# Attention scores in split float32r, transpositions of a slot first, and a written TensorE order, in a block-attention and gated-MLP kernel

## The chip, the cores and the metric

The kernel runs on one core of one Trainium2 chip. The metric is the device time of one execution in microseconds; lower is better. An execution under the hardware profiler gives the profile and the trace; times are in microseconds unless marked ns.

## The reference

Per batch (8) and head (8), with 576 positions of 64 values, the reference computes attention that is causal by blocks of 64. The eight heads are then laid side by side as 512 features, and a gated MLP with a mix over positions follows.

```python
scores = scale * np.matmul(q, k.transpose(0, 1, 3, 2))
mask = block_i >= block_j
scores = np.where(mask, scores, -1000000000.0)
scores = scores - np.max(scores, axis=-1, keepdims=True)
attn = np.exp(scores)
attn = attn / (np.sum(attn, axis=-1, keepdims=True) + 1e-09)
return np.matmul(attn, v).astype(np.float32)
...
h = x @ w_in
h = 0.5 * h * (1.0 + np.tanh(c * (h + 0.044715 * h ** 3)))
u, v = (h[..., :d_ff // 2], h[..., d_ff // 2:])
v_n = (v - mu) / np.sqrt(var + 1e-06) * g_ln
v_s = np.einsum('ts,bsd->btd', w_sg, v_n) + b_sg[None, :, None]
gated = u * v_s
return (x + gated @ w_out).astype(np.float32)
```

All inputs and outputs are float32, but the MLP's weights, which the kernel converts itself. The host only lays data out: q and k arrive transposed (64 values by 576 positions a head), and the output leaves transposed.

## The kernel before

**Pairs and slots.** Two heads of one batch make a pair, so there are 32 pairs. Their q and k lie one head in partitions 0 to 63 and the other in 64 to 127. One iteration of the last loop (L720) is a slot: it finishes the values' products of pair n (class Values) and makes the scores of pair n + 1 (class Scores). Four slots are one batch.

**Scores.** A pair has five row tiles: tile 0 has 64 rows, tiles 1 to 4 have 128, and tile i sees 64 + 128 i columns. `products` (L280) multiplies in fp32, one product for each head and part; the trace shows each fp32 product as two records, one for each of its two passes over the moving columns. `maximum` (L293) is one VectorE operation that adds the mask, scales, writes the scores to SBUF and takes the row's extreme; `exponent` (L308) is one ScalarE operation that also gives the row's sum. A slot has four score steps (L329 to L339): tile 4's first half with tile 1, tile 4's second half, tile 3 with tile 0, tile 2. Four sets of probability tiles (L149) let two pairs be alive at once.

**Values.** The probabilities are transposed by TensorE against an identity (L353) in three groups a head (`turn0`, `turn2`, `turn1`, L362 to L387), each into one PSUM bank that ScalarE or VectorE copies out (table TE, L341). A diagonal tile is transposed in its lower 64 rows alone, so the tile shape on the array changes there from 128 by 128 to 64 by 128. `turn_sums` (L405) transposes the inverse sums, which POOL has spread over 64 columns a head (L395). The values' products `av0`, `av2`, `av1` (L420 to L435) multiply fp32 values (the stationary operand, 64 columns a head) with the transposed probabilities, for both heads into the two halves of one bank. `normalise` (L437) multiplies by the inverse sums and spills the result; `split` (L445) splits it in a high float32r part and the rest, for the MLP.

**Feed-forward.** The MLP is a chain of generators that yields after each accumulated bank: 5 steps of `v_part` (products of 512 columns), 8 of `u_part`, 8 of `s_part` (the mix over positions) and 8 of `o_part`, all as sums of three float32r products of split operands with 288 columns, but v. `hole(k)` (L643) runs the next k steps; they stand in the slots where TensorE would otherwise have little, by the table PLAN (L660). The order of the parts is v, u, the output of the batch before, s. The norm between v and s (moments, centring, scaling, splitting) is a list of small steps, `side`, that `run_side(k)` (L459) issues k at a time; GELU is one entry of it for `run_gelu`. Weights arrive as 64-bit floats and are taken apart by three VectorE operations (L183, L184, L187), ScalarE and POOL in steps that `load_share` spreads by the table WS (L652).

**What sets the order.** The program is written for a planner: it simulates the engines and issues each engine's instructions in the order in which they become ready by its own costs. `tc.keep_in_program_order` (L82) binds an instruction to the written order; `PIN` (L57) is empty here, so TensorE's instructions are planned freely. PSUM has two rings: five banks "s" for scores, accumulators and outputs, three banks "p" for transpositions. All loads and stores are issued from SP's queue.

## Time and profile before

| | us |
|---|---|
| median of 3 runs | 1051.23 (1049.72 to 1056.15) |
| span of the profiled execution | 1050.8 |
| TensorE, matmuls | 964.7 busy, 5554 records |
| VectorE | 465.9 busy |
| ScalarE | 427.0 busy |
| POOL | 267.4 busy |
| HBM traffic | 45.78 MB read, 18.87 MB written, 62 GB/s over the span |

The profiled execution took 1050.75. "PE" is TensorE's matmuls, "PEld" its weight loads, DVE VectorE, ACT ScalarE, POOL GpSimd, SP the queue that issues the transfers. A tile's name stands with the operand it is written from: `s<-k_f,q_f` is a score product, `ob<-pt,v_f` a values' product, `pa`, `pb`, `pc`, `pd`, `pe` are the banks of transpositions, `accv`, `accu`, `accs` and `acco` the feed-forward accumulators. Matmuls are pipelined, so a record lasts longer than the step from its start to the next one's; the steps are what the engine's time is made of.

### The profile page before, as it was taken

What the parts mean: (1) busy time and instruction counts of PE and PEld (TensorE: products, weight loads), DVE (VectorE), ACT (ScalarE), POOL (GpSimd) and SP (SyncE); (2) the same over time, 40 slices, a digit from 0 to 9 for tenths busy, and PEclk for the clock granted to TensorE, in tenths of its full rate; (3) what the DMA queues carried; (4) which work ended last, traced back from release to release, by engine and by line L of the source; (5) the groups of instructions that cost most, each with busy time, mean ns of one, the idle gap of its engine ahead of it and who ended that gap; (6) DMA issues with size and microseconds to landing.
All of it is one profiled execution on the core that took longest, in us unless ns stands there. A gap on an engine that the chain in (4) does not pass through costs nothing.

```text
span 1050.8 us, 15018 instructions
## 1 busy us (share of the span) xinstructions
PE 964.7 (92%) x5554; PEld 690.3 (66%) x5554; DVE 465.9 (44%) x1442; ACT 427.0 (41%) x1122; POOL 267.4 (25%) x341
## 2 busy tenths in 40 slices
PE   8699999998889988999889998899988999889988
PEld 4245767576657765677666776567765577658978
DVE  6855285427334273342722526434263342723333
ACT  5765662562253622536224263243632536322210
POOL 3621064104212042120420303302042020422232
PEclk7799999998989989899878999889989899869999
DMA  7522111112210122101220112211122011112022
GB/s 233 167 91 68 56 56 46 46 46 68 95 34 31 46 68 90 46 22 46 68 80 34 46 47 68 79 35 46 46 68 88 27 44 58 34 39 75 1 90 68
DMA packets 46908, 65.61 MB, mean 62 GB/s; under 512 B 4082, under 2 KB 22514, under 8 KB 46836
## 3 DMA queue, kind: packets, MB, share of 16 engines
q1 hardware_dynamic: 46836, 64.67, 18.8%
q8 instruction: 43, 0.70, 0.3%
q14 instruction: 29, 0.24, 0.1%
HBM read 45.78 MB, written 18.87 MB: 62 GB/s over the span
## 4 chain that ended last, share of the span: by engine, by line
PE 76%; DVE 13%; ACT 3%; DMA 2%; POOL 2%; issue 2%; SPq 1%; DVEq 0%; POOLq 0%; ACTq 0%
PE s L85 12%; PE accs L85 12%; PE acco L85 11%; PE ob L85 11%; PE accv L85 10%; PE accu L85 9%; PE pc L88 3%; PE pb L88 3%; DVE prob L297 3%; PE pa L88 2%; DVE bs L518 2%; DVE xr L635 2%; ACT prob L310 1%; PE pe L88 1%; DMA w<-in_w_in 1%
## 5 line engine op out<-in xcount | busy, mean ns | idle before, releaser
L310 ACT ACTIVATE prob<-prob,negm 128x448 f32<-128x448 f32 (+3 forms) x320 | 177.8, 556 | 235.5 <-DVE negm L297 234.1
L85 PE MATMUL s<-k_f,q_f 64*128 64x288 f32 (+4 forms) x768 | 193.9, 447 | 34.2 <-DVE negm L297 23.7
L297 DVE CUSTOM_DVE_ANT_0 prob<-s,mask 128x288 f32<-128x288 f32 (+2 forms) x320 | 122.2, 424 | 168.9 <-PE s L85 168.8
L85 PEld LDWEIGHTS s<-k_f,q_f 64*128 64x128 f32 (+1 forms) x768 | 88.9, 188 | 102.1 <-issue 40.3
L85 PE MATMUL ob<-pt,v_f 128*64 128x448 f32 (+4 forms) x640 | 129.5, 454 | 11.0 <-ACT pt L92 6.6
L85 PE MATMUL acco<-gh,wo_h 128*128 128x288 f32 x256 | 94.2, 369 | 19.5 <-DVE xr L635 10.9
L273 POOL MEMSET sums<- 128x2 f32 x32 | 4.3, 137 | 353.1 <-DVE r L392 353.1
L611 POOL TENSOR_TENSOR gl<-u,gh 128x288 fp32r<-128x288 f32 x64 | 51.6, 807 | 154.6 <-DVE gh L610 151.9
L85 PEld LDWEIGHTS ob<-pt,v_f 128*64 128x64 f32 x640 | 44.1, 141 | 69.2 <-issue 39.7
L85 PE MATMUL acco<-gl,wo_h 128*128 128x288 f32 x256 | 87.1, 340 | 0.0
L85 PE MATMUL acco<-gh,wo_l 128*128 128x288 f32 x256 | 86.6, 338 | 0.0
L635 DVE TENSOR_TENSOR xr<-acco,xr 128x288 f32<-128x288 f32 x64 | 29.0, 456 | 121.1 <-PE acco L85 113.5
L85 PEld LDWEIGHTS acco<-gh,wo_h 128*128 128x128 f32 x256 | 58.9, 230 | 31.8 <-DVE xr L635 16.6
L85 PE MATMUL accu<-xh,wi_h 128*128 128x288 f32 x256 | 79.1, 309 | 0.0
L85 PE MATMUL accs<-ws_h,vh 128*128 128x288 f32 x256 | 76.8, 303 | 1.5 <-ACT pt L92 1.5
L85 PE MATMUL accs<-ws_h,vl 128*128 128x288 f32 x256 | 75.9, 297 | 0.0
L85 PE MATMUL accu<-xh,wi_l 128*128 128x288 f32 x256 | 75.5, 295 | 0.0
L85 PE MATMUL accu<-xl,wi_h 128*128 128x288 f32 x256 | 75.4, 295 | 0.0
L85 PE MATMUL accs<-ws_l,vh 128*128 128x288 f32 x256 | 75.1, 294 | 0.0
L85 PE MATMUL accv<-wi_h,xh 128*128 128x512 f32 x160 | 66.0, 413 | 0.0
L92 ACT COPY pt<-pa 128x512 f32<-128x512 f32 x32 | 18.6, 581 | 110.8 <-PE pa L88 110.8
L85 PE MATMUL accv<-wi_l,xh 128*128 128x512 f32 x160 | 63.4, 396 | 0.0
(102 smaller groups left out, 1839.8 us busy)
## 6 DMA issues: line engine op xcount, KB each, us to landing
q_f<-in_qT SPq DMA_DIRECT2D x32, 288.0 KB, 2.9
k_f<-in_kT SPq DMA_DIRECT2D x32, 288.0 KB, 3.2
spill<-x SPq DMA_DIRECT2D x32, 288.0 KB, 3.2
xr<-spill SPq DMA_DIRECT2D x32, 288.0 KB, 2.8
out_T<-xr SPq DMA_DIRECT2D x32, 288.0 KB, 2.1
v_f<-in_v SPq DMA_DIRECT2D x32, 256.0 KB, 3.1
w<-in_w_in SPq DMA_DIRECT2D x16, 256.0 KB, 4.7
w<-in_w_out SPq DMA_DIRECT2D x8, 256.0 KB, 3.9
```

The source lines that it names most:

```text
L85: return pin(nc.tensor.matmul(*a, **k), "P")
L88: return pin(nc.tensor.transpose(out, in_, identity), "P")
L92: return f(dst, src)
L273: nc.gpsimd.memset(self.sm[:, 0, :], 1.0)
L297: nc.vector.tensor_tensor_reduce(self.prob[a][i][r, lo:hi], self.where[a, i, lo], mask[r, MW - (hi - lo) :] if 0 < i and hi == e else mask ...
L310: nc.scalar.activation(self.prob[a][i][r, :e], self.prob[a][i][r, :e], AF.Exp, bias=self.negm[a][r, i : i + 1], scale=-1.0, accum_out=self ...
L518: tc.keep_in_program_order(nc.vector.bn_stats(bs[:rows, :], x))
L611: nc.gpsimd.tensor_tensor(glo[:, ts], x, ghi[:, ts].bitcast(F32), op=ALU.subtract)
L635: nc.vector.tensor_tensor(x[:, ts], acc[:, :SH], x[:, ts], op=ALU.add)
```

## The change

- **Scores.** q and k of a pair are split once (new function `split_qk`) in a high float32r part and a rest. A product is the sum of three float32r products, high by high, rest by high, high by rest, written alternately for the two heads. The split is made by POOL (for the first pair by VectorE and ScalarE). Tile 0 is multiplied with 128 rows instead of 64. The four steps become two: `first` (tile 4's two halves, tiles 1 and 0) and `second` (tiles 3 and 2). There is one set of probability tiles instead of two, and one buffer each for raw and split q and k.
- **Transpositions.** All are 128 by 128. Per head they are grouped in A (tile 4, four column tiles), B and C (five each), and with the sums they stand at the start of the slot, with feed-forward steps between the groups; the scores of the next pair come after them. Of the six copies out, three go to ScalarE and three to VectorE.
- **Values' products.** They come in one visit, between the next pair's two score steps, in 15 pieces a head, one for each pair of row and column tiles, instead of 6.
- **Order and banks.** `PIN` is "P": TensorE runs in the written order. The two PSUM rings become one of eight banks.
- **Plan.** PLAN puts the parts of the MLP in whole slots: v in a batch's first slot, u, the earlier output and s in the next three, four steps of them at the slot's end. `run_side` hands out three steps at a time. WS gives the first four slots 2 weight steps each.

```diff
-    PIN = ""
+    PIN = "P"
...
-    def bank(tag, name, bufs):
-        return psum.tile([P, 512], F32, tag=tag, name=name, bufs=bufs)
...
+    def bank(name):
+        return psum.tile([P, 512], F32, tag="bank", name=name, bufs=8)
...
+    def split_qk(n):
+        out = []
+        for x, t in zip(raw.pop(n), "qk"):
+            hi = sp.tile([P, S], F32R, tag=t + "h", name=t + "h", bufs=1)
+            lo = sp.tile([P, S], F32R, tag=t + "l", name=t + "l", bufs=1)
+            if n == 0:
+                copy("v" if t == "q" else "a", hi, x)
+                nc.vector.tensor_tensor(lo, x, hi.bitcast(F32), op=ALU.subtract)
+            else:
+                copy("g", hi, x)
+                nc.gpsimd.tensor_tensor(lo, x, hi.bitcast(F32), op=ALU.subtract)
+            out += [hi, lo]
+        qk[n] = out
...
-                    mm(dst, self.q[r, QS[i] : QS[i] + n], self.k[r, lo:hi], start=True, stop=True)
+                for y, (q, k) in enumerate(
+                    ((self.qh, self.kh), (self.ql, self.kh), (self.qh, self.kl))
+                ):
+                    for a in (0, 1):
+                        r = slice(a * D, (a + 1) * D)
+                        mm(
+                            t[a][:, cols],
+                            q[r, QS[i] : QS[i] + P],
+                            k[r, lo:hi],
+                            start=y == 0,
+                            stop=y == 2,
+                        )
...
+        def first(self):
             self.step((4, 0, SH), (1, 0, EXT[1]))
+            self.step((4, SH, S), (0, 0, EXT[0]))
+
+        def second(self):
+            self.step((3, 0, EXT[3]))
             self.step((2, 0, EXT[2]))
...
+    TE = {(0, "A"): "a", (1, "A"): "v", (0, "B"): "a", (1, "B"): "v", (0, "C"): "v", (1, "C"): "a"}
+    PLACES = {
+        "A": ((4, 0, 0), (4, 1, 128), (4, 2, 256), (4, 3, 384)),
+        "B": ((4, 4, 384), (3, 3, 320), (3, 2, 256), (3, 1, 128), (3, 0, 0)),
+        "C": ((1, 1, 384), (1, 0, 320), (2, 2, 192), (2, 1, 128), (2, 0, 0)),
+    }
...
+        def turn(self, a, which):
+
+            t = bank("p" + which)
+            for i, j, c in PLACES[which]:
+                turn(t[:, c : c + P], prob[a][i][:, P * j : P * (j + 1)])
+            pt = sp.tile([P, 512], F32, tag="pt", name="pt" + which, bufs=6)
+            copy(TE[a, which], pt, t)
+            for i, j, c in PLACES[which]:
+                self.pt[a, i, j] = pt[:, c + BLK : c + P] if i == j else pt[:, c : c + P]
...
+            t, t2 = bank("pd"), bank("pe")
             for a in (0, 1):
+                turn(t[:, a * BLK : a * BLK + P], prob[a][0])
+            for i in (0, 1, 2):
+                c = 2 * BLK + (i and BLK + P * (i - 1))
+                turn(t[:, c : c + P], spread(i))
+            for i in (3, 4):
+                turn(t2[:, P * (i - 3) : P * (i - 2)], spread(i))
...
+            self.o0 = t2[:, 2 * P : 2 * P + BLK]
+
+        def products(self):
+
+            self.ob = bank("ob")
+            for i in (4, 3, 2, 1, 0):
+                for j in range(i + 1):
+                    c = BLK if i == j and i else 0
+                    w = BLK if i == j else P
+                    c += P * (i - 1)
+                    for a in (0, 1):
+                        r = slice(a * D, (a + 1) * D)
+                        dst = self.ob[r, c : c + w] if i else self.o0[r, :]
+                        mm(
+                            dst,
+                            self.v[:, j, r],
+                            self.pt[a, i, j],
+                            start=j == 0,
+                            stop=j == i,
+                        )
 
         def normalise(self):
 
             x = self.x = page(F32, S, "x")
+            nc.vector.tensor_tensor(x[:, BLK:], self.ob, self.rb[:, BLK:], op=ALU.mult)
             nc.vector.tensor_tensor(x[:, :BLK], self.o0, self.rb[:, :BLK], op=ALU.mult)
-            nc.vector.tensor_tensor(x[:, BLK:], self.ob, self.rb[:, BLK:], op=ALU.mult)
...
-    WS = [2, 5, 7, 8, 3, 2, 1, 1]
+    WS = [2, 2, 2, 2, 8, 2, 2, 2, 4, 4]
...
-    PLAN = ["12211", "12211", "12211", "12222"]
+    PLAN = ["1112", "2114", "2114", "2114"]
...
         va.inverse()
+        va.turn(0, "A")
+        va.turn(1, "A")
         hole(g[0])
+        run_side(3)
         for f in pending:
             f()
         pending.clear()
+        va.turn(0, "B")
+        va.turn(1, "B")
         hole(g[1])
+        run_side(3)
+        load_share(n, 0)
+        va.turn(0, "C")
+        va.turn(1, "C")
+        va.turn_sums()
+        hole(g[2])
         run_gelu()
         load_share(n, 1)
         if nx:
+            nx = Scores(n + 1)
+            nx.first()
+        va.products()
+        va.normalise()
+        if nx:
+            nx.second()
         load_share(n, 2)
+        if n % 4 == 3:
+            va.split()
+        else:
+            pending.append(va.split)
+        if n + 2 < N:
+            split_qk(n + 2)
+        for _ in range(g[3]):
+            hole()
+            run_side(3)
         load_share(n, 3)
```

More of the change, by code (lines that the diff above doesn't have):

```diff
@@ L85, in mm, with turn @@
         return pin(nc.tensor.matmul(*a, **k), "P")
-    def turn(out, in_, identity):
-        return pin(nc.tensor.transpose(out, in_, identity), "P")
+    def turn(out, in_):
+        return pin(nc.tensor.transpose(out, in_, ident), "P")
     def copy(e, dst, src):
@@ L102, in load_qk @@
         b, h = PAIRS[n]
-        q_f = sp.tile([P, S], F32, tag="q_f", name="q_f", bufs=2)
-        k_f = sp.tile([P, S], F32, tag="k_f", name="k_f", bufs=2)
+        q_f = sp.tile([P, S], F32, tag="q_f", name="q_f", bufs=1)
+        k_f = sp.tile([P, S], F32, tag="k_f", name="k_f", bufs=1)
         nc.sync.dma_start(q_f, qT[b, h : h + 2].rearrange("a d s -> (a d) s"))
         nc.sync.dma_start(k_f, kT[b, h : h + 2].rearrange("a d s -> (a d) s"))
-        qk[n] = (q_f, k_f)
+        raw[n] = (q_f, k_f)
+    def split_qk(n):
[11 more added lines that the diff above has]
+        qk[n] = out
     def load_v(n):
@@ L124 @@
     make_identity(nc, ident)
-    t = sbank("warm")
+    t = bank("warm")
     for _ in range(18):
@@ L142 @@
         v_bufs.append(t)
-    pt0 = []
+    prob = []
     for s in (0, 1):
-        t = cp.tile([P, 2 * BLK], F32, name=f"pt0_{s}")
-        nc.gpsimd.memset(t[BLK:, :], 0.0)
-        pt0.append(t)
-    prob = []
-    for s in range(4):
         row = []
         for i in range(NT):
-            t = cp.tile([P, P * (i + 1) if i else BLK], F32, name=f"prob{s}_{i}")
+            t = cp.tile([P, P * (i + 1)], F32, name=f"prob{s}_{i}")
             if i:
                 nc.gpsimd.memset(t[:, EXT[i] :], 0.0)
+            else:
+                nc.gpsimd.memset(t, 0.0)
             row.append(t)
@@ L276, in __init__ @@
             ]
-            self.prob = prob[n % 2 * 2 : n % 2 * 2 + 2]
             self.where = {}
         def products(self, *parts):
-            t = [sbank("s"), sbank("s")]
+            t = [bank("s"), bank("s")]
             off = 0
             for i, lo, hi in parts:
-                n, rows = QN[i], slice(0, QN[i])
+                cols = slice(off, off + hi - lo)
                 for a in (0, 1):
-                    r = slice(a * D, (a + 1) * D)
-                    dst = t[a][rows, off : off + hi - lo]
-                    self.where[a, i, lo] = dst
-                    mm(dst, self.q[r, QS[i] : QS[i] + n], self.k[r, lo:hi], start=True, stop=True)
+                    self.where[a, i, lo] = t[a][: QN[i], cols]
+                for y, (q, k) in enumerate(
[10 more added lines that the diff above has]
+                        )
                 off += hi - lo
@@ L297, in maximum @@
             nc.vector.tensor_tensor_reduce(
-                self.prob[a][i][r, lo:hi],
+                prob[a][i][r, lo:hi],
                 self.where[a, i, lo],
@@ L310, in exponent @@
             nc.scalar.activation(
-                self.prob[a][i][r, :e],
-                self.prob[a][i][r, :e],
+                prob[a][i][r, :e],
+                prob[a][i][r, :e],
                 AF.Exp,
@@ L400, in turn_sums, with spread @@
         def turn_sums(self):
-            t = self.t4 = pbank("pd")
+            def spread(i):
+                return self.rx[:, i, :]
+            t, t2 = bank("pd"), bank("pe")
             for a in (0, 1):
-                turn(t[:BLK, a * BLK : (a + 1) * BLK], self.prob[a][0][:BLK, :BLK], ident[:BLK, :BLK])
-            turn(t[:, 128:256], self.rx[:, 0, :], ident)
-            pt = self.pt0 = pt0[self.n % 2]
-            copy("a", pt[:BLK, :], t[:BLK, : 2 * BLK])
-            self.rb = sp.tile([P, S], F32, tag="rb", name="rb")
@@ L409, in turn_sums @@
-            copy("a", self.rb[:, :BLK], t[:, 128:192])
-            t = pbank("pe")
-            for i in range(1, NT):
-                turn(t[:, (i - 1) * P : i * P], self.rx[:, i, :], ident)
-            copy("a", self.rb[:, BLK:], t)
-        def av(self, dst, j, pts, c0, n, start, stop):
-            for a in (0, 1):
-                r = slice(a * D, (a + 1) * D)
-                mm(dst[r, :], self.v[:, j, r], pts[a][:, c0 : c0 + n], start=start, stop=stop)
-        def av0(self):
-            self.ob = sbank("ob")
-            pt = [self.pt.pop((a, 0)) for a in (0, 1)]
-            self.av(self.ob, 0, pt, 0, 512, True, False)
@@ L477, in accumulator @@
     def accumulator(name):
-        return sbank(name)
+        return bank(name)
     def feed_forward(b):
@@ L490, in v_part @@
         x_s = xs[b]
-        for st in (NT - 1, *range(NT - 1)):
+        for st in range(NT):
             rows = P if st < NT - 1 else TAIL
@@ L507, in v_part @@
             else:
[L508 removed]
+                vt = sp.tile([P, DH], F32, tag="pt", name="vt", bufs=6)
                 nc.scalar.copy(vt[:TAIL, :], acc[BLK:, :])
@@ L713 @@
     load_v(0)
+    split_qk(0)
     load_qk(1)
     sc = Scores(0)
-    sc.step1()
-    sc.step2()
-    sc.step3()
-    sc.step4()
+    sc.first()
+    sc.second()
+    split_qk(1)
     for n in range(N):
```

107 lines of the change are left out of this document (18 added, 89 removed).

## The prediction

> **What bounds the kernel now.** I read the page first, then the busy time by stage, then the chain that ended last inside one steady batch.
>
> ```profile
> span 1050.8 us, 15018 instructions
> PE 964.7 (92%) x5554; PEld 690.3 (66%) x5554; DVE 465.9 (44%) x1442; ACT 427.0 (41%) x1122; POOL 267.4 (25%) x341
> PEclk7799999998989989899878999889989899869999
> PE 76%; DVE 13%; ACT 3%; DMA 2%; POOL 2%; issue 2%; SPq 1%; DVEq 0%; POOLq 0%; ACTq 0%
> ```
>
> TensorE is the bound: 92% busy, 76% of the chain. No other engine is half busy. So the question is what the change does to TensorE's own time and to its waits. By stage (columns: length; busy time of PE, PEld, DVE, ACT, POOL; granted clock; DMA):
>
> ```profile
> 0.00:98.40 98.40, 81.18 (x414) 42.72 (x414) 66.59 (x226) 62.60 (x185) 38.52 (x78) 0.84 0.47 149
> 98.40:200.30 101.90, 100.12 (x601) 67.16 (x597) 55.98 (x175) 54.77 (x142) 32.86 (x39) 1.00 0.17 53
> 67.50:80.50 13.00, 12.72 (x84) 6.72 (x83) 7.52 (x31) 8.48 (x28) 2.50 (x4) 1.00 0.29 92
> 600.10:729.70 129.60, 119.48 (x694) 85.72 (x693) 54.53 (x171) 51.73 (x135) 29.72 (x35) 0.93 0.17 56
> 974.10:1050.80 76.70, 68.17 (x458) 63.75 (x456) 25.88 (x57) 10.53 (x22) 19.88 (x21) 1.00 0.17 55
> ```
>
> The reader is to see five stages. Up to 98.4 there is attention of the first four pairs and the weights. 98.4 to 200.3 holds the first feed-forward parts, still without any output part. Then come steady batches of about 130 us (four slots each; 600.1 to 729.7 is one), and from 974.1 a tail of feed-forward alone. The third row is one early slot with attention only: 13.0 us at full clock. Four such slots are 52 us, so a batch of 129.6 leaves 78 for feed-forward. What does feed-forward itself need? From the chain in the steady batch (start, length, what):
>
> ```profile
> 607.79 3.70 PE accv L85 x15
> 611.49 0.44 PE pe L88 x4
> 627.81 3.38 PE accu L85 x24
> 632.21 1.40 PE pc L88 x9
> 638.50 1.02 PE ob L85 x8
> 683.70 1.80 PE acco L85 x12
> 709.61 11.34 PE accs L85 x84
> ```
>
> One step is 3.70/15 = 0.247 us for v, 3.38/24 = 0.141 for u, 0.150 for the output and 11.34/84 = 0.135 for the spatial product. A batch has 56, 96, 96 and 112 of them: 13.8 + 13.5 + 14.4 + 15.1 = **56.8 us**. Attention in a steady batch therefore costs 129.6 - 56.8 = 72.8 us, 18.2 a slot, against 13.0 in the early slot. The early slot shows why:
>
> ```profile
> 89.98 1.56 PE L85 MATMUL s<-k_f,q_f 64*128 64x288 f32 x12
> 642.95 1.07 PE L85 MATMUL s<-k_f,q_f 64*128 64x288 f32 x4
> 645.76 1.07 PE L85 MATMUL s<-k_f,q_f 64*128 64x288 f32 x4
> 67.50:80.50 13.00, 3.70 (x24) 1.00 0.29 92
> 600.10:729.70 129.60, 24.57 (x96) 0.93 0.17 56
> ```
>
> Early, twelve score passes (both heads) take 1.56 us, because the heads use different rows of the array and run together. In the steady batch the planner issues four passes of one head in 1.07 us, and four of the other almost 3 us later, with transpositions between. The last two rows are scores alone: 3.70 us in the early slot, 24.57/4 = 6.1 in a steady slot. The second loss is a stretch where VectorE leads:
>
> ```profile
> 642.00:660.00 18.00, 13.76 (x74) 9.71 (x74) 17.01 (x38) 4.73 (x13) 10.93 (x11) 0.81 0.12 39
> 651.15 1.99 POOL rs L530
> 653.54 1.12 PE L88 MATMUL pe<-ident,rx 128*128 128x128 f32 x4 [0.60 <-DVE x L440]
> ```
>
> For 18 us VectorE is 94% busy with the moments and centring of the norm, mixed with maxima and divisions; TensorE gets its work late and its clock falls (mean 0.81): four transpositions take 1.12 us, tail included.
>
> **The change, part by part.** Per slot, at full clock.
>
> Transpositions: 35 before, 35 after, all now 128 by 128. A plain one steps 0.44/4 = 0.110 us. The nine of the pc row would be 0.99 and take 1.40: 0.41 for four changes of tile shape, 0.10 each. After: 35 x 0.110 = **3.9 us**, no change inside.
>
> Scores: 12 fp32 products in two passes become 36 float32r products, 18 pairs. No row shows a 64-row float32r product. Per column it is bounded below by accu's 288 columns in 0.141 for a pair that runs together as the early fp32 passes do, and above by the same for each head alone. I take the pair, since the row with 1.56 us shows two heads together. A short product is charged a transposition's step, 0.110. Widths 448, 320, 288, 288, 192, 64: 0.22 + 0.16 + 0.14 + 0.14 + 0.11 + 0.11 = 0.88, times three terms = **2.6 us**; unpaired 5.2.
>
> Values' products: same 1600 columns a head in two passes, in 15 pieces rather than 6. 638.50 shows 512 columns in two passes in 1.02 us, so 1600 take at most 3.2; I take **3.0**, since that row carries its own start once, and the whole comes in one visit. If every piece paid a weight load of 0.110 for its 30 passes that would be 3.3, so the upper end is near.
>
> Changes of shape: feed-forward to scores, to values, to scores, to feed-forward: 4 x 0.10 = **0.4**.
>
> The new wait: TensorE keeps the written order, and all tiles share a ring of eight banks. The second score step's second bank is the one that holds the first rows' output, released by the last multiplication of the division, and behind it in TensorE's order stand all the holes. These rows price it, with the rest of the work that is moved:
>
> ```profile
> 664.08 0.70 DVE x L441
> 664.78 0.04 issue
> 664.83 1.28 PE s L85 x4
> L441 DVE TENSOR_TENSOR x<-ob,rb 128x512 f32<-128x512 f32 x32 | 22.1, 692 | 70.3 <-PE ob L85 65.2 <-issue 3.6 <-ACT rb L92 0.9
> L440 DVE TENSOR_TENSOR x<-pd,rb 128x64 f32<-128x64 f32 x32 | 6.9, 215 | 3.2 <-ACT prob L310 2.0 <-PE pd L85 1.1
> L297 DVE CUSTOM_DVE_ANT_0 prob<-s,mask 128x448 f32<-128x448 f32 x64 | 39.7, 621 | 39.0 <-PE s L85 38.9
> L310 ACT ACTIVATE prob<-prob,negm 128x448 f32<-128x448 f32 x64 | 42.6, 665 | 63.6 <-DVE negm L297 62.8
> L453 POOL TENSOR_TENSOR xl<-x,xh 128x576 fp32r<-128x576 f32 x32 | 45.7, 1427 | 0.0
> L395 POOL COPY rx<-r 128x640 f32<-128x640 f32 x32 | 23.6, 738 | 91.2 <-PE pe L88 58.7 <-DVE r L393 26.2 <-DVE negm L297 6.3
> L183 DVE TENSOR_SCALAR w<-w 128x256 uint32<-128x256 uint32 x24 | 10.5, 436 | 12.5 <-DMA w<-in_w_in 9.7 <-DMA w<-in_w_out 2.7
> L184 DVE SCALAR_TENSOR_TENSOR w<-w 128x256 uint32<-128x256 uint32 x24 | 13.4, 564 | 0.2
> L187 DVE SCALAR_TENSOR_TENSOR w<-w 128x256 uint32<-128x256 uint32 x24 | 12.3, 517 | 1.4 <-ACT w L181 1.3
> ```
>
> The first three rows are such a hand-over today: scores start 0.05 us after the division ends. So the two multiplications, 0.69 + 0.22, and two hand-overs are 1.0 us at least. Before them VectorE has the first step's eight maxima, under 4 us in all, while the 3.0 us of values' products run; where they come late, or a feed-forward step stands between, the wait grows. I take **1.5 us** a slot, between 1.0 and 4.
>
> Splitting q and k: on POOL two copies (0.74 x 576/640 = 0.67) and two subtractions (1.43): 4.2 us a slot. POOL has 29.7/4 = 7.4 busy a slot, so 11.6 of about 26: covered by the four holes (7 us) and the next slot up to its scores. If POOL fell behind, the transposed sums would be late, and with them everything on TensorE. Loads of q and k have one buffer, and on SP's queue they wait for that split, a few us into the slot; the loads of the residual stand behind them and have a hole's time to spare. The exponentials of the second step (four, 0.67 + read-out or less each) lie under the holes before the slot that transposes them.
>
> Sum of attention per slot: 3.9 + 2.6 + 3.0 + 0.4 + 1.5 = 11.4, 45.6 a batch; with 56.8 it is 102.4. The norm's VectorE work is now handed out three steps a hole; I leave 4 us of its 18 as lateness: **106 a batch**.
>
> The stages. Prologue: 22 weight steps stand in the first four slots now, 8 after. One costs VectorE 0.44 + 0.56 + 0.52 = 1.5 us, so 21 us leave a stretch where weights and first scores share VectorE. A slot with attention only cannot be hidden by holes: second scores, maxima, exponentials, sums on POOL behind the split, transposed sums, first scores and values follow each other; some 15 us against 13. So 98.4 - 21 + 8 = **85**. Next four slots: v 25, u 25, then s directly after u without an output part between, so its norm chain is open for some 8 us: 34; then an empty one of 15: **99** against 101.9. Six batches, 636, less 3 since the last slot has no scores: **633**. Tail unchanged: **77**. Together 894 of span 1050.8; the median shown, 1051.23, is 0.4 above the profiled span. **Forecast: 895 us.**
>
> A rule against the change, to be weighed: in the profile above a slot with 35 transpositions ran at clock 1.00 (67.5 to 80.5). The Trainium skill, page "TensorE: Matmul & The Clock Gate", section "Part 4: PE-mode transpose", says that a transposition doesn't count as a busy array for the clock gate. By it, seventeen in one run, as the change writes them, would lower the clock; the row speaks against it, though that slot has no run of seventeen. The rule stands behind rival (c).
>
> **The rivals.** (a) Float32r heads don't run together: 2.6 us more in 32 slots, 83: **978**. For it: the pairing is seen here for fp32 alone. Against: it is two row groups, not a number format. (b) The written order keeps the stretch where VectorE leads: the whole 18 us in seven batches instead of 4, so 7 x 14 = 98: **993**. For it: the same norm work, and TensorE can't step aside any more. Against: it is spread over two slots, and VectorE is 42% busy. (c) Slower: the clock. TensorE's visit of scores and values with its forced stop, and the runs of transpositions, drop it to half, as from 642 to 660. All attention work, 9.9 us a slot, at half clock adds 9.9 x 32 = 317: **1210**. It decides from half of that on (156 us, the gain). For: stops now block TensorE. Against: holes of dense products stand between, and early slots hold 1.00 without any. (d) The written order binds TensorE alone and other queues' planned orders stop it about as often as now: no gain, **1050**.
>
> **How the numbers follow.** Forecast 0.60, (a) 0.09, (b) 0.22, (c) 0.06, (d) 0.03. The likeliest's own range, 845 to 945, comes from 0.5 us less or 4 us at the new wait and a prologue of 75 to 100. The full range takes in (a) and (b): 845 to 1000. Faster by over 1% (what measurement here tells from no change): 0.60 + 0.09 + 0.22 = 0.91; within 1%: 0.03; slower 0.06.
>
> **What would show it.** Score pairs start together in every slot, with steps near 0.14 for 288 columns; batches near 106; transpositions step 0.110 in runs of eight to seventeen; a wait of 1 to 2 us on the division before the second scores; first feed-forward product near 85; clock near 1.0 in steady batches. Wrong it would be if TensorE's idle time per batch stayed above 25 us, if the heads' scores ran one after the other, or if the clock fell in the visits.

## The result and the profile after

The changed kernel takes **813.62 us** (median of 4 runs, 812.15 to 814.23) against 1051.48 for the kernel before (4 runs, 1049.72 to 1056.15): a ratio of 0.7753, 95% interval 0.7711 to 0.7795. The forecast was 895 with a range of 845 to 1000. The direction was right, the gain (238 us) was half as large again as the 156 forecast, and the range missed it by 31 us.

The page of the changed kernel, in the lines that answer to those shown of before:

```profile
span 812.0 us, 18284 instructions
PE 761.3 (94%) x7090; PEld 714.0 (88%) x7090; DVE 480.9 (59%) x1477; ACT 411.4 (51%) x1061; POOL 397.0 (49%) x457
PEclk8699997599999999999999999999999999999999
PE 86%; DVE 5%; POOL 3%; DMA 2%; issue 2%; ACT 1%; DVEq 0%; SPq 0%; POOLq 0%
```

TensorE is still the bound, and more so: 86% of the chain instead of 76%, though the trace has 1536 more records of its products. After the eighth of the forty slices its granted clock is full (1.00 from 159.5 us to the end of the work), where before showed dips to the end. By stage (length; busy time of PE, PEld, DVE, ACT, POOL; granted clock; DMA), with the prologue, slots 4 to 7, one steady batch and the tail:

```profile
0.00:84.20 84.20, 57.55 (x587) 49.29 (x587) 61.35 (x199) 49.84 (x148) 42.94 (x75) 0.86 0.43 130
84.20:189.50 105.30, 86.00 (x791) 78.69 (x789) 58.96 (x175) 54.19 (x138) 53.82 (x58) 0.87 0.23 71
467.20:559.70 92.50, 92.50 (x887) 87.69 (x886) 55.23 (x176) 49.24 (x127) 46.67 (x52) 1.00 0.25 78
741.00:812.00 71.00, 66.29 (x458) 63.52 (x456) 25.41 (x57) 12.43 (x23) 19.79 (x21) 1.00 0.18 59
```

| stage | before | forecast | after |
|---|---|---|---|
| to the first v product | 98.4 | 85 | 84.2 |
| slots 4 to 7 | 101.9 | 99 | 105.3 |
| steady batches | 773.8 | 633 | 551.5 |
| tail | 76.7 | 77 | 71.0 |

The steady row is 741.0 - 189.5 after and 974.1 - 200.3 before. It carries 222 of the 239 us between the spans, and 81.5 of the 82 by which the forecast's 894 was too long. In the third row of the fence PE is busy for 92.50 of 92.50 us at clock 1.00: a steady batch has no wait left. One whole slot of it, from the chain that ended last (start, length, what):

```profile
489.43 0.87 PE pA L75 x8
490.30 3.18 PE accu L72 x24
493.48 1.09 PE pB L75 x10
494.57 1.59 PE accu L72 x12
496.16 1.09 PE pC L75 x10
497.25 0.55 PE pd L75 x5
497.80 0.22 PE pe L75 x2
498.02 1.60 PE accu L72 x12
499.62 1.58 PE s L72 x24
501.20 2.80 PE ob L72 x56
504.00 0.12 PE pe L72 x4
504.12 1.25 PE s L72 x12
505.36 6.56 PE accu L72 x48
511.92 0.87 PE pA L75 x8
```

Every piece begins where the one above ends; from 489.43 to 511.92 is 22.5 us. Ninety-six products of u are 3.18 + 1.59 + 1.60 + 6.56 = 12.9 us, transpositions 0.87 + 1.09 + 1.09 + 0.55 + 0.22 = 3.8, scores 1.58 + 1.25 = 2.8, values 2.80 + 0.12 = 2.9.

### The profile page after: what moved, and what is told of

It is laid out like the page before. It is cut to its first block, busy times and chain, and to the rows that moved or that the text cites. A ratio compares the mean times of both kernels' runs of the same rounds, so it can differ in the third digit from the quotient of the medians.

```text
span 812.0 us, 18284 instructions
## 1 busy us (share of the span) xinstructions
PE 761.3 (94%) x7090; PEld 714.0 (88%) x7090; DVE 480.9 (59%) x1477; ACT 411.4 (51%) x1061; POOL 397.0 (49%) x457
## 4 chain that ended last, share of the span: by engine, by line
PE 86%; DVE 5%; POOL 3%; DMA 2%; issue 2%; ACT 1%; DVEq 0%; SPq 0%; POOLq 0%
PE accs L72 15%; PE accv L72 13%; PE accu L72 13%; PE acco L72 12%; PE ob L72 10%; PE s L72 10%; PE pC L75 4%; PE pB L75 4%; PE pA L75 3%; PE pd L75 2%; DVE prob L303 1%; DVE w L181 1%; ACT prob L316 1%; PE pe L75 1%; DVE w L182 1%
## 5 line engine op out<-in xcount | busy, mean ns | idle before, releaser
L316 ACT ACTIVATE prob<-prob,negm 128x576 f32<-128x576 f32 (+3 forms) x320 | 176.8, 554 | 86.5 <-DVE negm L303 83.5
L303 DVE CUSTOM_DVE_ANT_0 prob<-s,mask 128x288 f32<-128x288 f32 (+3 forms) x320 | 121.8, 424 | 61.8 <-PE s L72 61.1
L72 PE MATMUL acco<-gh,wo_h 128*128 128x288 f32 x256 | 77.8, 304 | 0.0
L594 DVE TENSOR_TENSOR u<-accs,u 128x288 f32<-128x288 f32 x64 | 29.3, 458 | 63.9 <-PE accs L72 63.2
L72 PEld LDWEIGHTS accs<-ws_h,vh 128*128 128x128 f32 x256 | 49.1, 192 | 18.9 <-DVE vh L526 15.7
L72 PE MATMUL s<-kh,qh 64*128 64x288 f32 (+4 forms) x384 | 63.3, 324 | 0.0
L79 POOL CAST kh<-k_f 128x576 fp32r<-128x576 f32 x31 | 21.1, 681 | 84.1 <-PE s L72 79.5
L72 PE MATMUL s<-kh,ql 64*128 64x288 f32 (+4 forms) x384 | 59.6, 305 | 0.8 <-POOL ql L106 0.8
L316 ACT ACTIVATION_READ_ACCUMULATOR prob<-prob,negm 128x1 f32 x320 | 59.8, 187 | 0.0
L72 PE MATMUL s<-kl,qh 64*128 64x288 f32 (+4 forms) x384 | 58.4, 302 | 0.0
```

The lines of the kernel that those rows point to most:

```text
L72: return pin(nc.tensor.matmul(*a, **k), "P")
L79: return f(dst, src)
L303: nc.vector.tensor_tensor_reduce(prob[a][i][r, lo:hi], self.where[a, i, lo], mask[r, MW - (hi - lo) :] if 0 < i and hi == e else mask[r, : ...
L316: nc.scalar.activation(prob[a][i][r, :e], prob[a][i][r, :e], AF.Exp, bias=self.negm[a][r, i : i + 1], scale=-1.0, accum_out=self.sm[r, i, ...
L594: nc.vector.tensor_tensor(x, acc[:, :SH], x, op=ALU.mult)
```

## The experiments

**The measure.** Besides the medians, each profile was reduced to what TensorE's time goes to in a steady batch: the time from one matmul's start to the next one's, less the part in which nothing ran, summed by what the matmul is for (mean of three batches). "Paired" is the share, over the whole run, of score records that start within 20 ns of another one; two that overlap with starts further apart don't count. "First v" is the end of the prologue, "last v" the start of the tail (both are starts of the feed-forward's v part).

| run | median us | ratio to before, 95% | batch | scores | values | transp. | feed-f. | idle | paired | first v | last v |
|---|---|---|---|---|---|---|---|---|---|---|---|
| before | 1051.5 | 1 | 132.0 | 23.7 | 15.2 | 21.4 | 61.4 | 10.2 | 0.48 | 98 | 974 |
| h2_side_two | 1036.2 | 0.987 (0.976 to 0.999) | 128.7 | 23.4 | 15.1 | 20.9 | 60.3 | 9.1 | 0.49 | 99 | 959 |
| h1_one_ring | 946.7 | 0.902 (0.890 to 0.914) | 114.4 | 17.9 | 16.3 | 18.7 | 56.8 | 4.6 | 0.67 | 99 | 872 |
| h8_ring_tile0 | 934.3 | 0.887 (0.874 to 0.899) | 112.9 | 16.3 | 16.1 | 18.7 | 56.4 | 5.1 | 0.56 | 96 | 860 |
| h4_scores_together | 969.1 | 0.921 (0.914 to 0.927) | 114.2 | 19.2 | 19.3 | 18.0 | 55.4 | 2.2 | 0.57 | 108 | 899 |
| h5_one_visit | 931.2 | 0.885 (0.879 to 0.891) | 112.8 | 22.4 | 12.8 | 17.5 | 57.9 | 2.2 | 0.51 | 94 | 860 |
| h6_written | 898.5 | 0.853 (0.841 to 0.865) | 106.9 | 18.0 | 11.4 | 17.5 | 57.0 | 3.0 | 0.87 | 87 | 825 |
| h7_whole_tile0 | 899.2 | 0.853 (0.841 to 0.865) | 108.1 | 18.3 | 12.8 | 17.5 | 57.2 | 2.3 | 0.54 | 91 | 828 |
| e8_fp32_planned | 824.5 | 0.782 (0.771 to 0.793) | 96.6 | 13.0 | 11.7 | 14.5 | 55.3 | 2.0 | 0.98 | 77 | 752 |
| e3_fp32_scores | 833.6 | 0.793 (0.788 to 0.799) | 96.1 | 12.6 | 11.7 | 14.5 | 55.2 | 2.0 | 0.99 | 80 | 762 |
| after | 813.6 | 0.775 (0.771 to 0.780) | 92.5 | 11.3 | 11.7 | 14.3 | 55.2 | 0.0 | 0.99 | 84 | 741 |
| e1_planned | 811.9 | 0.773 (0.765 to 0.781) | 92.5 | 11.3 | 11.7 | 14.3 | 55.2 | 0.0 | 0.97 | 87 | 738 |
| e4_heads_apart | 816.0 | 0.777 (0.769 to 0.785) | 92.5 | 11.4 | 11.7 | 14.3 | 55.2 | 0.0 | 0.94 | 85 | 743 |
| e5_half_rows | 854.8 | 0.814 (0.808 to 0.821) | 97.9 | 11.3 | 11.7 | 19.0 | 55.9 | 0.0 | 1.00 | 86 | 779 |
| g1_two_rings | 819.9 | 0.781 (0.772 to 0.790) | 93.3 | 11.4 | 11.7 | 14.4 | 55.2 | 0.7 | 0.99 | 84 | 748 |
| g2_side_all | 812.8 | 0.774 (0.766 to 0.783) | 92.5 | 11.3 | 11.7 | 14.3 | 55.2 | 0.0 | 1.00 | 84 | 740 |
| x1_two_visits | 822.7 | 0.781 (0.776 to 0.785) | 93.8 | 12.0 | 12.3 | 14.3 | 55.2 | 0.0 | 1.00 | 87 | 751 |
| e6_s_later | 811.1 | 0.771 (0.767 to 0.774) | 92.5 | 11.3 | 11.7 | 14.3 | 55.2 | 0.0 | 1.00 | 84 | 738 |
| e9_first_fp32 | 810.6 | 0.775 (0.770 to 0.780) | 92.5 | 11.3 | 11.7 | 14.3 | 55.2 | 0.0 | 1.00 | 81 | 739 |
| e10_mixed | 798.6 | 0.763 (0.758 to 0.768) | 92.4 | 11.3 | 11.7 | 14.3 | 55.2 | 0.0 | 0.99 | 79 | 725 |

From before to after a batch falls by 39.5 us: scores 12.4, values 3.5, transpositions 7.1, feed-forward 6.2 (the same products, less of them at half clock), idle 10.2.

**The theories.** The first was the prediction's: TensorE's written order puts the heads' scores side by side and keeps them so. Its rivals: the shapes alone do it (every product of a group has one shape, so that any order pairs); the one ring of eight banks does it, in place of five for work and three for transpositions; the finer handing-out of the norm's small steps does it; the format does it.

### Changes taken out of the changed kernel

**The written order undone.**

```diff
-    PIN = "P"
+    PIN = ""
```

> The changed kernel, but TensorE's order left to the planner. Theory (the written order is the larger part of the gain, since it keeps the two heads' scores together and never stops TensorE in a steady batch): steady batches of 105 to 120 us instead of 92.5, in all 890 to 980 us, with score products of the two heads apart again and TensorE idle 5 us or more a batch. Rival (the new shapes and the three-term scores are the gain, the order is not): 800 to 830 us.

811.85 us, nothing lost: the first theory fell. The planner's order differs from the written one, and one slot of its chain is as tight:

```profile
496.85 1.58 PE s L72 x24
498.43 2.80 PE ob L72 x56
501.23 0.12 PE pe L72 x4
501.35 1.25 PE s L72 x12
```

The same 1.58, 2.80 and 1.25 us, and 97% of the score products still paired, in steady batches all of them.

**The heads' products written one head after the other.**

```diff
-                for y, (q, k) in enumerate(
-                    ((self.qh, self.kh), (self.ql, self.kh), (self.qh, self.kl))
-                ):
-                    for a in (0, 1):
+                for a in (0, 1):
+                    for y, (q, k) in enumerate(
+                        ((self.qh, self.kh), (self.ql, self.kh), (self.qh, self.kl))
+                    ):
```

> The changed kernel with the three terms of one head written before those of the other, instead of alternately; same products. Theory (two heads in different rows of the array run at the same time only when they are next to each other in the order): scores go from 2.85 to about 5.0 us a slot, 2.2 us in 31 slots, in all 870 to 885 us. Rival (the array takes the second head early anyway): below 825 us.

816.02, within the interval of after. The instructions do stand three of one head, then three of the other, as a wait in the prologue shows. There the second terms wait for a split. In after the heads' first products start together ahead of that wait (62.708 and 62.711); here the first head's starts at 64.582 and the second head's only at 65.257, behind the first head's waiting one (65.251). The trace of a steady slot of this run (start, length, instruction; x2 is two records laid together) shows how they ran:

```profile
501.32 0.41 PE L72 MATMUL s<-kh,qh 64*128 64x288 f32 x2
501.55 0.30 PE L72 MATMUL s<-kh,ql 64*128 64x288 f32 x2
501.68 0.31 PE L72 MATMUL s<-kl,qh 64*128 64x288 f32 x2
```

In each row one product is of the first head and one of the second; the two of the first row start at 501.318 and 501.328. The second head's first product, written fourth, started before the first head's second. So in a steady batch even the order within a group of one shape costs next to nothing (scores 11.4 instead of 11.3).

**Scores as they were in number format, without the split.**

```diff
-        out = []
-        for x, t in zip(raw.pop(n), "qk"):
...
-        qk[n] = out
+        qk[n] = raw.pop(n)
...
+                for a in (0, 1):
+                    r = slice(a * D, (a + 1) * D)
+                    mm(t[a][:, cols], self.q[r, QS[i] : QS[i] + P], self.k[r, lo:hi], start=True, stop=True)
```

(the raw q and k also have two buffers each instead of one)

> The changed kernel with the scores as fp32 products again (two passes, heads still written alternately), without the splitting of q and k. Theory (float32r gives TensorE almost nothing here: a pair of 288 columns takes three steps of 0.13 us as float32r and two of 0.24 as fp32, 0.39 to 0.48): steady batch 92.5 plus 0 to 2 us, in all 805 to 830 us, POOL some 125 us less busy. Rival (three fast terms instead of two double passes are a main source): scores 5.7 us a slot as in the steady batch before, 880 us or more.

833.62, just above the range of the theory: the format with its split is worth 20 us. Scores are 12.6 against 11.3 a batch; 2.0 of idle come back, one wait a batch, for an output part (us in all, times, longest):

```profile
PE acco L72 <- DVE xr L600: 12.2, 6, 2.0
```

**The same scores with the planner's order.**

```diff
-    PIN = "P"
+    PIN = ""
```

> The changed kernel with fp32 scores and TensorE's order left to the planner (with the written order 833.6 us, 99% of the score records beside the other head's). Theory shape (all scores have one shape here): 90% or more and 825 to 842 us. Theory order: 80% or less and 850 us or more.

824.54, and 98% paired. The two intervals overlap, so the 9 us between them are not told from nothing. Neither the format nor the order is what made the heads run together.

**Diagonal transpositions from 64 rows again.**

```diff
-                turn(t[:, c : c + P], prob[a][i][:, P * j : P * (j + 1)])
+                if i == j:
+                    pin(nc.tensor.transpose(t[:, c + BLK : c + P], prob[a][i][BLK:, P * j : P * (j + 1)], ident[BLK:, BLK:]), "P")
+                else:
+                    turn(t[:, c : c + P], prob[a][i][:, P * j : P * (j + 1)])
```

> The changed kernel with the eight diagonal transpositions of a slot (B and C of both heads) taken from 64 rows again. Theory (a change of tile shape costs 0.10 us, a transposition of 64 rows 0.055 instead of 0.110): twelve changes cost 1.2 us, eight shorter transpositions save 0.44, so 0.7 to 0.8 us a slot in 28 slots that TensorE bounds, in all 830 to 836 us. Rival (the changes cost nothing in a written order): 800 us.

854.81: 41 us lost, twice what was expected, and most of it by transpositions (14.3 to 19.0 a batch). The chain of this run shows the price of a change of shape (L365 are the half ones, L75 the whole ones):

```profile
519.96 0.20 PE pC L365
520.17 0.26 PE pC L75
520.42 0.20 PE pC L365
520.63 0.37 PE pC L75 x2
```

These five transpositions take 1.03 us with four changes of shape among them; five whole ones in a run take 0.55 (0.109 each). That is 0.12 a change. Over the whole batch it is 5.4 us for 48 changes, 0.11 each. And a half one saves nothing: in the trace of before two of them, one behind the other, start 0.111 us apart (632.616 and 632.727), as whole ones do, not half of that as was expected here.

**Values' products in two visits.**

```diff
-            nx.first()
-        va.products()
+            nx.step((4, 0, SH), (1, 0, EXT[1]))
+        va.products((4,))
+        if nx:
+            nx.step((4, SH, S), (0, 0, EXT[0]))
+        va.products((3, 2, 1, 0))
```

> The changed kernel with the values' products in two visits, tile 4 between the next pair's first two score parts and the rest after them: two more changes of tile shape a slot, nothing else. Theory C: 0.10 to 0.15 us a change, 0.2 to 0.3 us a slot in 28 slots, in all 818 to 823 us. Rival (the array changes shape behind running work, and the cost in the diagonal transpositions was something else): 811 to 815 us.

822.66. The slowest run of after (814.23) and the fastest of this (820.24) are 6 us apart, though the intervals of the ratios overlap; what the edit costs is read from the pieces. A slot has two more changes of shape:

```profile
506.55 0.91 PE s L72 x12
507.46 1.14 PE ob L72 x20
508.60 0.85 PE s L72 x12
509.45 1.81 PE ob L72 x36
```

Scores 0.91 + 0.85 against 1.58 in one visit, values 1.14 + 1.81 against 2.80: 0.33 us for two changes, 0.16 each.

**Two rings of banks again; the norm's small steps handed out without limit.**

```diff
-        return psum.tile([P, 512], F32, tag="bank", name=name, bufs=8)
+        t, n = ("p", 3) if name[0] == "p" else ("s", 5)
+        return psum.tile([P, 512], F32, tag=t, name=name, bufs=n)
```

> The changed kernel with the old two PSUM rings, five banks for scores, accumulators and outputs, three for transpositions. Theory A: TensorE gets its waits back, steady batch 92.5 to 98 or more, in all 850 to 900 us. Theory B, and the rival that TensorE is so far behind every other engine that three banks less do nothing: 808 to 825 us.

```diff
-        run_side(3)
+        run_side(99)
```

(at its four places)

> The changed kernel with all the norm's small steps handed out at once at the first place, instead of three at a time. Theory B: VectorE's block of some 18 us stands before maxima and divisions again, steady batch up by 5 to 15 us, in all 845 to 915 us. Theory A: 808 to 825 us, as the holes of feed-forward steps cover it.

819.94 and 812.84; both intervals overlap that of after. Two rings put 0.7 us of idle into a batch and no more.

### Changes put into the kernel before

**One ring of banks; fewer of the norm's small steps at a time.**

```diff
-        return bank("s", name, 5)
+        return bank("b", name, 8)
...
-        return bank("p", name, 3)
+        return bank("b", name, 8)
```

> The kernel before, with one PSUM ring of eight banks for scores, accumulators and transpositions instead of five and three. The written order is out as a cause, so theory A (the five-bank ring parted the two heads' scores and let TensorE wait on maxima and divisions): steady batch 129.6 down to 112 to 120, scores of a steady slot from 6.1 towards 4 us, in all 950 to 1000 us. Theory B (VectorE's norm work stands in front of maxima and divisions, whichever bank they hold): 1035 to 1055 us.

```diff
-        run_side(4)
+        run_side(2)
```

(at its four places)

> The kernel before, with the norm's small steps handed out two at a time instead of four. Theory B (18 us of a steady batch are led by VectorE's norm block): the block spreads over twice the slots, batch down by 5 to 12 us, in all 970 to 1015 us. Theory A (banks): 1040 to 1055 us.

One ring alone takes 102 us off (946.65 against 1048.44 on the same chip). The norm's steps take some 12 (1036.16), with an interval that leaves anything from 2 to 25; the time lies between the ranges of the two theories. Four of TensorE's waits before (waited for: us in all, times, longest):

```profile
PE s L85 <- DVE negm L297: 23.7, 25, 4.1
PE acco L85 <- DVE xr L635: 10.9, 20, 1.6
PE acco L85 <- DVE negm L297: 8.5, 10, 1.4
PE s L85 <- DVE xr L635: 6.1, 11, 0.6
```

and with one ring:

```profile
PE s L85 <- DVE negm L297: 14.1, 9, 2.7
PE pa L88 <- DVE negm L297: 7.5, 5, 2.9
PE ob L85 <- ACT pt L92: 6.1, 3, 2.9
```

Before, scores and output products wait for VectorE to read an earlier bank (the maxima, the residual's sum), in 66 waits of 49 us; with eight banks for all the output products no longer stand in the list. The rest of the 102 goes with clock and pairing: feed-forward 61.4 to 56.8 a batch, with the granted clock of the steady batches up from 0.91 to 0.99, and scores 23.7 to 17.9. What cost 102 us in the old code costs 6 in the new, and those are not told from nothing. That feed-forward steps now stand between the groups of transpositions may be why; no run shows it.

**On one ring: scores' parts called together, then values' products in one visit.**

```diff
+            nx.step1()
+            nx.step2()
+            nx.step3()
```

(all behind the transposed sums; taken away at their old places)

> The kernel before with one ring of eight banks, and the next pair's four score steps in one place after the transposed sums instead of spread over the slot; products still fp32. With the ring alone it took 946.7 us, a steady batch 114.5, scores 18.5 of it. Theory C (what the ring leaves is the cost of visits: the two heads apart, and changes of tile shape): scores fall to about 13 us a batch, as fp32 scores in one place do in the changed kernel (12.6), batch to 108 or 109, in all 895 to 915 us. Rival (the score steps spread over the slot hide maxima and exponentials, and one place exposes them): 950 us or more.

```diff
-        va.av0()
...
-        va.av2()
...
+        va.av0()
+        va.av2()
```

(both now ahead of the last visit; transposed tiles six buffers instead of four, probabilities one set of tiles)

> As the one before, and the values' products in one visit at the slot's end (six buffers for the transposed probabilities, one set of probability tiles). Theory C: values' products from 16.9 to about 12 us a batch, as in the changed kernel, in all 855 to 885 us. Rival (visits of values' products cost nothing by themselves): within 10 us of the one before.

The first missed: 969.11, 22 us worse than one ring alone. Its batch is the same 114.2; the loss lies ahead of the steady batches (first v 108 instead of 99, first steady batch at 224 instead of 202). The second gained 38 over it but came short of its expectation as well: values fell from 19.3 to 12.8 a batch, scores rose to 22.4. The records of one step show why. Starts in us: the first head's 448 columns at 422.608 and 422.984 (two passes), its 64 x 64 product at 423.450, and only then the second head's 448 columns at 423.705. The small product has another tile shape and stands between the heads' long products, which don't meet. In h7, below, where it has the same shape, the two long ones start 7 ns apart at this step (411.469 and 411.476).

**On that: TensorE's written order, or tile 0 on the whole array.**

```diff
-    PIN = ""
+    PIN = "P"
```

> The old code with one ring, scores in one place and values in one visit, now with TensorE in the written order. Left to the planner it took 931.2 us, steady batch 113, scores 22.0 of it, with 51% of the score records starting beside the other head's. Theory order (the planner's order parts the heads): 90% or more beside each other, scores 13 to 15 us a batch, in all 865 to 890 us. Theory shape (the 64-by-64 product of tile 0 between two parts of 128 rows parts them): some 70%, scores 16 to 20 us, in all 890 to 925 us, as two changes of shape stay in each slot.

```diff
-                n, rows = QN[i], slice(0, QN[i])
+                rows = slice(0, QN[i])
...
-                    mm(dst, self.q[r, QS[i] : QS[i] + n], self.k[r, lo:hi], start=True, stop=True)
+                    mm(t[a][:, cols], self.q[r, QS[i] : QS[i] + P], self.k[r, lo:hi], start=True, stop=True)
```

> The old code with one ring, scores in one place and values in one visit, order left to the planner, and tile 0's scores taken over 128 rows (the upper 64 are not used), so that all score products have one shape. Theory shape: 75% or more of the score records beside the other head's, scores 14 to 18 us a batch, in all 880 to 910 us. Theory order: 45 to 55%, 925 us or more.

898.45 and 899.18: each is worth 32 to 33 us here, and both lie in the range of the theory of shapes. The written order does it by pairing (0.87, values 11.4). The whole tile 0 does it by changes of shape that fall away (scores 18.3), but its share of pairs stays at 0.54, where that theory expected 0.75 or more. The long products now meet, but their second passes start 0.11 us apart (411.845 and 411.955) and don't count as paired; and the planner puts values' products, of yet another shape, between the heads' next products, which start 1.0 us apart (412.847 and 413.837). So one shape for all scores isn't enough where the order is free and other shapes can come between; in the changed kernel, where a visit holds scores alone, the order made no difference (e1, e8). The second edit on one ring alone:

> The kernel before with one ring of eight banks and tile 0's scores over 128 rows, all else as before. With the ring alone 946.7 us and 67% of the score records beside the other head's. Theory shape: 75% or more, 920 to 938 us. Theory order or banks: 941 to 952 us.

934.28 against 946.65, with intervals that overlap: not told from nothing. The share of pairs fell from 0.67 to 0.56, against the 0.75 that was expected. The old kernel with the whole written order and nothing else was not tried, so what order alone does there stays open.

### What was left in the changed kernel

TensorE's longest stop after the change is in slot 6 (a wait as above, then the chain: start, length, what):

```profile
PE accs L72 <- DVE vh L526: 16.5, 4, 14.5
```

```profile
122.28 6.58 PE accu L72 x48
...
134.98 1.45 POOL ws_l L168
136.43 1.34 POOL rs L515
137.77 1.37 POOL ws_l L233
...
152.62 1.28 POOL vl L527
153.94 4.69 PE accs L72 x18
```

u ends at 128.9, eight transpositions follow until 129.7, and then TensorE stands for 14.5 us, until the first product of s at 144.2. From there to 153.9 it gets ten products, a few at a time as the norm hands over its tiles. In these 24 us POOL is busy for 12.7 with the norm (vv, vl, rs) and for 5.5 with weights, and VectorE for 5.4 with weights. The granted clock is at half from 132 to 159.

```diff
-        g = [int(x) for x in PLAN[n % 4]]
+        g = [1, 1, 1, 1] if n in (5, 6) else [int(x) for x in PLAN[n % 4]]
```

> The changed kernel with the first batch's feed-forward spread differently: four u steps each in slots 5 and 6 and the s steps in slot 7, instead of eight u steps in slot 5, s in slot 6 and nothing in slot 7. TensorE stood for 25 us in slot 6 waiting for POOL's and VectorE's norm chain, at half clock for 27. Theory (the s steps came one slot too early): that wait goes, slots 4 to 7 take 80 to 88 us instead of 105, in all 787 to 797 us. Rival (the chain on POOL is the bound in that stretch wherever the s steps stand): 808 us or more.

```diff
+        if n < 4:
+            qk[n] = raw.pop(n)
+            return
```

(scores of the first four pairs in one fp32 term; raw q and k two buffers each instead of one, the split x four instead of five)

> The changed kernel with the scores of pairs 0 to 3 as fp32 products without a split, all others as float32r (two raw buffers each for q and k, four instead of five buffers for the split x). With fp32 scores throughout, the first feed-forward product came at 80 instead of 84 us, with the planner's order at 77, and each later batch was 3.6 us longer. Theory (in slots of attention alone POOL's splitting stands in the chain from the sums to the next scores, in steady slots it is covered): 4 to 8 us less, 804 to 810 us. Rival (the gain there came from the double raw buffers or is given back by the fewer buffers of x): 811 us or more.

811.14 and 810.64. Neither is told from after. Putting u off moved the stop and shortened it (139.0 to 150.0, 11.0 us), but the norm's chain ended later too: the dense run of s starts at 161.0 instead of 153.9. The second edit brought the first v product 3 us forward, and the stop grew to 16.3. Both together with the planner's order:

> As the one before, with TensorE's order left to the planner and the u steps spread over slots 5 and 6 with s in slot 7. Each of the two alone measured 1 to 2.5 us less than the changed kernel. If the three savings add, 798 to 806 us; if the stretch from first attention to the first norm has one bound (VectorE and POOL with the weights), 804 to 812 us.

```profile
78.50:174.20 95.70, 84.93 (x791) 77.35 (x789) 63.18 (x182) 56.05 (x144) 55.34 (x61) 0.95 0.24 78
```

798.59 us, ratio 0.7629 (0.7578 to 0.768), 12 below e9 on the same chip and the fastest kernel of the study. Slots 4 to 7 take 95.7 instead of 105.3, at clock 0.95 instead of 0.87: the longest stop is 9.5 us, and the clock is at half behind it for 10 us instead of 27. The steady batch is untouched (92.4). The saving is more than that of its parts one by one; which pair of them does it was not separated.

## Why the prediction was right, and where it was wrong

**What failed: the steady batch, 106 against 92.5.** The terms of its sum, against the table's row (us a batch):

| term | forecast | measured |
|---|---|---|
| feed-forward | 56.8 | 55.2 |
| transpositions | 15.6 | 14.3 |
| scores | 10.4 | 11.3 |
| values | 12.0 | 11.7 |
| changes of shape | 1.6 | inside the others |
| new wait on the division | 6.0 | 0 |
| lateness of the norm | 4.0 | 0 |
| sum | 106.4 | 92.5 |

Ten of the 13.9 us are the two waits that did not come; the other 3.9 are small errors of the products' terms.

**The wait on the division** is the step that failed most clearly: 1.5 us a slot were charged for it. The prediction let the second scores' bank be the one that holds the first rows' output. The timeline of a steady slot (start, length, instruction, then idle before):

```profile
504.05 0.47 PE L72 MATMUL s<-kh,qh 64*128 64x448 f32 x2
...
504.21 0.69 DVE L425 TENSOR_TENSOR x<-ob,rb 128x512 f32<-128x512 f32 x1 [1.10 <-DMA v_f<-in_v]
...
504.82 0.21 DVE L426 TENSOR_TENSOR x<-pe,rb 128x64 f32<-128x64 f32 x1
```

The second scores start at 504.05, before the division even begins at 504.21; it ends at 505.03 and nobody on TensorE waits. So they wrote into another bank: the ring isn't walked in strict rotation, as the prediction assumed. That the planner gave out whichever bank was free is read from this, and has no run of its own.

**The lateness of the norm** (4 us a batch, and 18 in rival b) came to nothing: idle is 0.0 in the table. VectorE's share of the span rose from 44% to 59% all the same, so its load alone didn't make the stretch where it led. That TensorE now has other work to issue meanwhile is the likely reason; g2, with all of the norm's steps handed out at once, leaves idle at 0.0 as well.

**The sizes of the products** were right within 10%: pairs of 288 columns step 0.13 (499.783 to 499.910) where 0.14 was read from accu; 448 and 320 columns take 1.25 where 1.14 was worked out; values 2.92 where 3.0 was taken. **A change of shape** was put at 0.10 us from the pc row; e5 gives 0.11 to 0.12 between transpositions, x1 0.16 between scores and values. That didn't harm the forecast, which had four of them a slot.

**Prologue** 84.2 against 85: the number came right, its terms did not, so that is in part luck. The sum took off 14 weight steps, 21 us. But the planner pulled weight steps of later slots forward: VectorE did 16 of them in this stage and 20 before, and its work on w fell from 30.3 to 25.3 us. The first slot, which holds them, lasts 26 us instead of 35. The sum also charged 15 us for a slot of attention alone; such slots start 13.5, 14.2 and 12.7 us apart (pA at 42.9, 56.4, 70.6, 83.3). **Slots 4 to 7** 105.3 against 99: the empty stretch of slot 6 was named, and put at 8 us, for which no row was given; it is 24, and POOL's norm steps alone take 12.7 of it. The other terms came out shorter and hid most of that: by slot 22, 22, 50 and 11 us against 25, 25, 34 and 15. **Tail** 71.0 against 77: "unchanged" failed by 6 us, as TensorE's busy time fell by 1.9 and its idle time by 3.8; no run isolates why.

**The reason given** was only partly right. That it takes the written order to pair the heads fell with e1, e4 and e8. What the runs show to be worth time is one shape in a group (e5, h7), one visit (x1, h5) and, in the old code, one pool of banks (h1); the written order is worth 33 us in h6, where shapes are still mixed, and nothing in the changed kernel. The path from before to after, in steps that were run: one ring 102 us; scores' parts together with one visit 15 (946.65 to 931.19); tile 0 whole 32; the whole transpositions, the regrouped slot and the weight plan together 75 (899.18 to 824.54), of which e5 gives 41 to the transpositions and the first v 14 to the prologue; the format 11 to 20. The parts depend on one another (two rings: 102 or 6; order: 33 or 0), so this is one path and not a sum of independent prices.

**The rivals.** (a) fell: 99% of the products pair in float32r. (b) fell, above. (d) fell. (c), the clock at half, was right about what a stop does and wrong about where: after the prologue it happens once, in slot 6. The rule of the Trainium skill, page "TensorE: Matmul & The Clock Gate", section "Part 4: PE-mode transpose", that was weighed behind it would have the clock fall in runs of transpositions; in the slot shown, pC, pd and pe are seventeen in one run from 496.16 to 498.02, 0.109 us each, in a batch at clock 1.00. The longest run of this kind is in slot 7, 35 of them from 179.0 to 182.8, and the clock stays at 1.00 there too. These runs speak against the rule; in slot 6 the clock fell only 2.5 us after TensorE's last work (129.7 and 132.2), so a run of 3.8 us tests it, but not by much.

**What the list of signs told.** Paired starts, runs of transpositions at 0.110, the first v near 85 and the full clock came as listed; batches near 106 and the wait of 1 to 2 us did not. The list had no sign for "better than forecast". The range doesn't follow from its own terms either: 0.5 us less at the wait in 32 slots and a prologue of 75 give 895 - 16 - 10 = 869, and 4 us at the wait with a prologue of 100 give 895 + 80 + 15 = 990, where 845 and 945 were written. And even 845 had no room for the wait and the lateness both at nothing (10 us a batch, 60 in six batches).

## What to carry to other kernels

Give every product of a group one tile shape, even where this computes columns that nobody reads: here a change of shape cost 0.11 to 0.16 us, as much as a whole transposition or more, a transposition of half the rows was no shorter, and a product of another shape parted products that run together on two row groups. When a forecast adds a wait for a buffer, let the range reach to that wait at nothing unless the code fixes which buffer it is. A term that comes out right may still be two wrong ones: look at its parts. And credit an order only after a run without it: the part that carries the name of the change may be the one that does nothing.

## What the runs showed of the hardware

Products on different row groups don't keep the written order among themselves: in e4 the second head's first product, written fourth, started 10 ns behind the first head's first and ahead of its second and third (501.318, 501.328, 501.553). The Trainium skill, page "TensorE: Matmul & The Clock Gate", section "Part 3: Packing small matmuls — row/col tiling", has matmuls start and end in program order, with no reordering; by the starts of this trace they don't.

A product of another tile shape between them ends that: in h5 the heads start 1.1 us apart (422.608, 423.705), in h7 with one shape 7 ns at the same step (411.469, 411.476). An fp32 product of 64 rows and a float32r product in three terms are close in price where heads pair: 12.6 and 11.3 us a batch for scores, so the split's gain here (20 us) lies more in the 2.0 us of idle per batch than in the products.
